# Moving the last steps of a small MLP off VectorE in a one-core decode kernel

## Chip, core and metric

The kernel runs on one core of one Trainium2 chip. The metric is the device time of one execution in microseconds (us). The kernel before takes 193.9 us, the median of three runs (193.79 to 194.43). Engines are named as in the profile: PE (TensorE matmuls), PEld (weight loads of TensorE), DVE (VectorE), ACT (ScalarE), POOL (GpSimd) and SP (SyncE, which here only issues DMAs).

## What is computed

One token with 512 features is normalised. A branch A is attention over the last 4096 positions of a cache of 32 heads with 128 features each. A branch B is a small MLP with two residual steps and a silu at its end. The result is x plus the product of both. Cut to what matters:

```python
xn = layernorm(x)                                   # 1 x 512
q  = xn @ wq                                        # 32 heads x 128
p  = softmax(q . k_cache[:, -4096:] / sqrt(128))
s  = (p . v_cache[:, -4096:]) @ wo                  # 1 x 512

x1 = xn + shift(gelu(layernorm(xn) @ w1)) @ w2      # one token: the shift leaves zeros
h2 = gelu(layernorm(x1) @ w3) @ w4
g  = silu(x1 + h2)
out = x + s * g
```

Keys, values and weights are bf16. Keys and values of the window are 32 MB each, and all bytes are read once: 78.8 MB.

## The kernel before

**Staging.** The 32 heads are worked in 8 groups of 4. A group's keys are one block of 128 partitions x 128 columns x 128 features (4 MB), as are its values. Three key blocks fit on the chip (`K_BUFS = 3`) and two value blocks (`V_BUFS = 2`). All big transfers but wq are issued by SP in program order (`load`, L75), and an issue waits until its buffer is free. The first key block comes in two halves of 64 columns, the last value block in four pieces (columns 0 to 64, 64 to 96, 96 to 112, 112 to 128, `cuts`, L570), followed by the last rows of wo (`load_rows`). The value pool is opened in the space of the pool `wts` (L580), so the first value load waits until the last reader of `wts` tiles is done; `hr` (L279) is one of those tiles.

**Scores.** The columns of a group are shared between two ways. VectorE takes the first 64 to 80 columns (`nd`) in four parts (`k_vector`): a product of keys and the spread query (L338), and a sum over features (L340). PE and ScalarE take the rest in batches: PE transposes keys (`k_turn`, L356), ScalarE copies them from PSUM (L359), and PE multiplies with the query (`k_scores`, L367). Then come own scores (L376), the maximum (`sm_max`, L381 and L383), its turning across partitions (`sm_turn`, L389, L391, L393), the exponentials (`sm_exp`, L398 to L405), the denominators (`sm_den`, `sm_rden`, L411 and L416), and the weighted values (`v_wide`, L444, with the eviction L450; turning L461 and L466). The groups overlap with a lag of two steps (`LAG`).

**Order.** From L571 on the order on PE, VectorE and ScalarE is written out by hand, step by step. In step 7 PE turns the maximum of group 6 (L389) after VectorE's L416, since both use the single buffer of the PSUM pool `ps_misc`. After the last step: the last value block is used piece by piece (`v_wide` and `v_part`, L477), the output projection of the early heads is turned and multiplied with `g_own` (`y_turn`, L556 to L561), and the last four heads follow in `y_head` (L549), sixteen small products. `g_own` is read a second time in L697, and L700 and L701 add x and store. The calls of `warm` put in matmuls of zeros whose result nobody reads.

**The MLP's end** (L269 to L296) stands ahead of that region; there a scheduler orders each engine's instructions, and it sets those of VectorE between the first products of group 0. Four row groups of PSUM collect the wide row (`hr_ps`). VectorE copies it to SBUF (`hr`, L280), PE turns it into columns with four products against `ind` (L283, f32, eight passes in the profile), VectorE adds `xn_col` (L285), ScalarE takes the silu (L287), and VectorE spreads the result over a mask, 128x16, as `g_own` (L295). `hr_ps` and `h2_ps` use the one buffer of `ps_misc`, so PE's products also wait for the copy of `hr_ps`.

Of the kernel before, what the change touches and what calls it, by code (L numbers as in the profile page):

```python
# [8 lines left out]
P = 128  # L9
BF16 = mybir.dt.bfloat16  # L10
FP32 = mybir.dt.float32
ACT = mybir.ActivationFunctionType
ALU = mybir.AluOpType
# [13 lines left out]
def kernel(  # L27
# [14 lines left out]
    nc = tc.nc  # L42
# [11 lines left out]
    KC = D // P  # L54
# [9 lines left out]
    small = ctx.enter_context(tc.tile_pool(name="small", bufs=1))  # L64
# [10 lines left out]
    def load(dst, src):  # L75
# [7 lines left out]
                        in_=A_wq.rearrange("(a b c) n -> b a (c n)", a=4, c=KC))  # L83
# [19 lines left out]
    ident_f = const.tile([P, P], FP32, name="ident_f")  # L103
# [13 lines left out]
    ind = const.tile([P, 1], FP32, name="ind")  # L117
# [28 lines left out]
    def ln_stats(src_f, tag):  # L146
# [30 lines left out]
                     start=True, stop=True)  # L177
# [23 lines left out]
    for b in range(2):  # L201
        zeros(qr[b][:])
        for c in range(KC):
            wc = wq_sb[:, c, :].rearrange("p (g a d) -> p g a d", a=G, d=Dh)
            for a in range(G):
                nc.tensor.matmul(qr[b][32 * a:32 * a + 1], lhsT=xq_bf[:, c:c + 1], rhs=wc[:, 4 * b:4 * b + 4, a, :],  # L206
                                 start=False, stop=(c == KC - 1), skip_group_check=True)
    nc.scalar.copy(out=q_row[:, 0:4, 0, :], in_=qr[0][:])  # L208
    nc.vector.tensor_copy(out=q_row[:, 4:8, 0, :], in_=qr[1][:])  # L209
    for b in range(2):  # L210
        qb_ps = ps_tr.tile([P, 4, Dh], FP32, tag="pt", name="qb_ps")
        nc.tensor.matmul(qb_ps[:], lhsT=sel[:].rearrange("k b a -> k (b a)"), rhs=q_row[:, 4 * b:4 * b + 4, 0, :],
                         start=True, stop=True)
        nc.scalar.copy(out=q_bc[:, 4 * b:4 * b + 4, :], in_=qb_ps[:])
    for b in range(2):
# [5 lines left out]
        for t in range(2):  # L221
            rows = slice(64 * t, 64 * t + 64)
            nc.scalar.copy(out=q_pair[rows, 4 * b:4 * b + 4, :, G * t:G * t + G].rearrange("p g l a -> p g a l"),
                           in_=qt_ps[rows].bitcast(BF16).rearrange("p g (a m l) -> p g a m l", a=G, l=2)[:, :, :, 0, :])
# [4 lines left out]
    for j in range(KC):  # L229
        for c in range(KC):  # L230
            nc.tensor.matmul(hs_ps[:, j:j + 1], lhsT=w2_sb[:, c, j::4],
                             rhs=shifted_bf[:, c:c + 1], start=(c == 0), stop=(c == KC - 1))
# [12 lines left out]
                            in1=r_slot[:].unsqueeze(2).to_broadcast([XR, KC, XC]), op=ALU.mult)  # L245
    xt_ps = ps_misc.tile([P, KC], FP32, tag="misc", name="xt_ps")
    nc.tensor.matmul(xt_ps[:], lhsT=r_in[:].rearrange("k a n -> k (a n)"), rhs=r_row[:], start=True, stop=True)
    xn_col = small.tile([P, KC], FP32, name="xn_col")
# [5 lines left out]
    for c in range(KC):  # L254
# [3 lines left out]
        for j, dst, w in parts:  # L258
            nc.tensor.matmul(dst, lhsT=z3_bf[:, c:c + 1], rhs=w, start=False, stop=(c == KC - 1),
                             skip_group_check=True)  # L260
# [8 lines left out]
    hr_ps = ps_misc.tile([P, KC, P], FP32, tag="misc", name="hr_ps")  # L269
    zeros(hr_ps[:])  # L270
    terms = [(shifted_bf[:, c:c + 1], w2_sb[:, c, :]) for c in range(KC)]
    for i in range(11):
        n = P if i < 10 else 96
        terms.append((a_bf[0:n, i % 3, i // 3:i // 3 + 1], w4_sb[0:n, i, :]))
    for i, (col, w) in enumerate(terms):
        r = 32 * (i % 4)
        nc.tensor.matmul(hr_ps[r:r + 1].rearrange("r j n -> r (j n)"), lhsT=col, rhs=w, start=False,
                         stop=(i >= len(terms) - 4), skip_group_check=True)
    hr = wts.tile([P, D], FP32, name="hr")  # L279
    nc.vector.tensor_copy(out=hr[:], in_=hr_ps[:].rearrange("p j n -> p (j n)"))  # L280
    h2_ps = ps_misc.tile([P, KC], FP32, tag="misc", name="h2_ps")
    for j in range(KC):
        nc.tensor.matmul(h2_ps[:, j:j + 1], lhsT=hr[:, j * P:(j + 1) * P], rhs=ind[:], start=True, stop=True)  # L283
    bv = small.tile([P, KC], FP32, name="bv")
    nc.vector.tensor_tensor(out=bv[:], in0=xn_col[:], in1=h2_ps[:], op=ALU.add)  # L285
    g_col = small.tile([P, KC], FP32, name="g_col")
    nc.scalar.activation(out=g_col[:], in_=bv[:], func=ACT.Silu)  # L287


    make_masks(16)  # L290
# [1 line left out]
    make_masks(4)  # L292
    NQ = P // XC
    g_own = small.tile([P, KC, NQ], FP32, name="g_own")
    nc.vector.tensor_tensor(out=g_own[:], in0=g_col[:].unsqueeze(2).to_broadcast([P, KC, NQ]),  # L295
                            in1=masks[4][2][:].unsqueeze(1).to_broadcast([P, KC, NQ]), op=ALU.mult)  # L296
    fold_f = const.tile([P, XC], FP32, name="fold_f")
    nc.vector.tensor_reduce(out=fold_f[:], in_=ident_f[:].rearrange("d (i t) -> d t i", t=XC), axis=AX.X, op=ALU.max)
# [7 lines left out]
                     skip_group_check=True)  # L306
# [7 lines left out]
                            op=ALU.max)  # L314
    par_t = const.tile([1 + G, PB, G], FP32, name="par_t")
    nc.vector.tensor_scalar(out=par_t[:],
                            in0=ident_f[0:1 + G, 1:1 + G].unsqueeze(1).to_broadcast([1 + G, PB, G]),
# [202 lines left out]
                                    op=ALU.add)  # L520
        ox_blk[i] = ox

    small.tile([P, 48], BF16, name="pad_rows")
    y_sum = small.tile([P, D], FP32, name="y_sum")
    small.tile([P, 32], BF16, name="pad_result")

# [205 lines left out]
```

## Time and profile before

| | |
|---|---|
| median of three runs | 193.9 us (193.79 to 194.43) |
| the profiled execution | 193.44 us |
| its span, first to last instruction | 191.6 us |
| busy: PE / DVE / ACT / POOL | 123.0 / 155.0 / 89.1 / 2.2 us |
| DMA | 79.02 MB, mean 412 GB/s |
| mean granted clock of TensorE | 0.666 |
| costliest group: L340 on DVE, 32 times | 87.6 us |
| L338 on DVE, 32 times | 46.1 us |
| L359 on ACT, 51 times | 50.0 us |
| L280 on DVE, once | 0.68 us |

The page gives the busy share of each engine in 40 equal slices of the span (4.79 us each) as digits in tenths, the chain of work that ended last, followed back from the last instruction, and groups of instructions by line. A timeline gives each instruction's start, duration, engine, line, tiles and shapes; in brackets stands how long its engine sat idle before it and what released it. For a DMA the time from issue to landing is given; landing is issue plus that time. "Room" below is the time between the landing of data and the start of the first instruction that reads it.

### The profile page before, as it was taken

To read this page: it belongs to the slowest core of one execution; us is meant where nothing else is said; L and a number is where in the kernel's file an instruction comes from. 1 tells how busy PE (TensorE), PEld (TensorE's weight loads), DVE (VectorE), ACT (ScalarE), POOL (GpSimd) and SP (SyncE) were. 2 spreads that over 40 slices of the span, in tenths; PEclk is the share of its full clock that TensorE was granted. 3 is DMA by queue.
4 is the path that set the end of the run, shared out by engine and by line. 5 is a ranking of instruction groups with operands and counts; after the bars stand their busy time and mean duration, and the time that the engine had idled before them with its cause. 6 is when DMAs were issued, how large, how long until landed. Compare 5 with 4: busy or idle time off the path is not lost.

```text
span 191.6 us, 2818 instructions
## 1 busy us (share of the span) xinstructions
PE 123.0 (64%) x1141; PEld 78.5 (41%) x1141; DVE 155.0 (81%) x187; ACT 89.1 (46%) x191; POOL 2.2 (1%) x10
## 2 busy tenths in 40 slices
PE   2545956778656069626944694566867396877983
PEld 1321316566545054414433443432653184533342
DVE  4730168999999999999999999999999999982021
ACT  2000741978587065807481737372755157653120
POOL 2110000000000000000000000000000000000000
PEclk9999695555555555855695558557655858585798
DMA  6999999999999999999999998999999999999980
GB/s 218 450 410 433 446 427 460 417 417 417 427 439 438 431 438 427 438 438 438 434 438 438 438 427 380 469 438 431 421 424 439 417 431 404 455 438 409 412 339 5
DMA packets 4621, 79.02 MB, mean 412 GB/s; under 512 B 544, under 2 KB 1152, under 8 KB 1664
## 3 DMA queue, kind: packets, MB, share of 16 engines
q1 hardware_dynamic: 4432, 74.65, 91.3%
q10 hardware_dynamic: 176, 4.20, 5.1%
q8 instruction: 9, 0.15, 0.3%
q14 instruction: 4, 0.03, 0.0%
HBM read 78.84 MB, written 0.00 MB: 411 GB/s over the span
## 4 chain that ended last, share of the span: by engine, by line
DVE 70%; PE 14%; DMA 9%; ACT 4%; issue 1%; ACTq 0%; DVEq 0%
DVE S L340 42%; DVE prod L338 21%; DMA wq_sb<-in_A_wq_dram 9%; PE ov L444 3%; PE yr_ps L543 2%; PE qr_ps L206 2%; PE pt L356 1%; DVE m L383 1%; DVE S L381 1%; PE h_ps L283 1%; PE wm L532 1%; PE ot_ps L461 1%; ACT kt L359 1%; DVE mx L391 1%; ACT L287 1%
## 5 line engine op out<-in xcount | busy, mean ns | idle before, releaser
L340 DVE TENSOR_REDUCE S<-prod 128x20 f32<-128x2560 bf16 (+2 forms) x32 | 87.6, 2736 | 1.1
L359 ACT COPY kt<-pt 128x1024 bf16<-128x1024 bf16 (+1 forms) x51 | 50.0, 1004 | 45.3 <-PE pt L356 43.6
L356 PE MATMUL pt<-ident_f,kv 128*128 128x128 f32 x202 | 47.3, 388 | 5.0 <-DMA kv<-in_A_k_cache_dram 5.0
L338 DVE TENSOR_TENSOR prod<-kv,q_bc 128x2560 bf16<-128x2560 bf16 (+2 forms) x32 | 46.1, 1442 | 2.2 <-ACT q_row L216 2.1
L356 PEld LDWEIGHTS pt<-ident_f,kv 128*128 128x128 f32 x202 | 35.0, 204 | 8.3 <-DMA kv<-in_A_k_cache_dram 6.1
L367 PE MATMUL sT<-q_pair,kt 128*128 128x8 bf16 x404 | 19.1, 171 | 15.5 <-ACT kt L359 15.3
L367 PEld LDWEIGHTS <-kt 128*128 128x128 bf16 x404 | 16.5, 106 | 26.2 <-ACT kt L359 25.1
L444 PE MATMUL ov<-kv,pT 128*16 128x512 bf16 x248 | 23.9, 551 | 0.0
L389 PE MATMUL mt_ps<-ident_f,m 128*1 128x128 f32 x8 | 3.0, 372 | 21.4 <-DVE rden L416 19.5
L405 ACT ACTIVATE pT<-S,mb 128x128 bf16<-128x128 f32 x32 | 13.9, 573 | 0.2
L450 ACT COPY ov_sb<-ov 128x512 f32<-128x512 f32 x8 | 4.7, 586 | 19.4 <-PE ov L444 19.4
L444 PEld LDWEIGHTS <-pT 128*16 128x16 bf16 x248 | 7.0, 116 | 13.9 <-issue 13.0
L389 PEld LDWEIGHTS mt_ps<-ident_f,m 128*1 128x1 f32 x8 | 0.6, 79 | 22.1 <-DVE rden L416 20.1
L376 ACT ACTIVATE own<-sT,par 128x48 f32<-128x48 f32 (+2 forms) x32 | 7.4, 352 | 3.7 <-PE sT L367 3.7
L461 PE MATMUL ot_ps<-ident_f,ov_sb 128*128 128x128 f32 x32 | 7.5, 377 | 1.8 <-ACT mb L401 1.5
L208 ACT CAST q_row<-qr_ps 128x512 bf16<-128x512 f32 x1 | 0.6, 585 | 17.0 <-PE qr_ps L206 17.0
L405 ACT ACTIVATION_READ_ACCUMULATOR pT<-S,mb 128x1 f32 x32 | 8.3, 258 | 0.0
L209 DVE CAST q_row<-qr_ps 128x512 bf16<-128x512 f32 x1 | 0.7, 691 | 9.1 <-PE qr_ps L206 9.1
L398 PE MATMUL mb_ps<-md,par_t 5*128 5x4 f32 x16 | 4.3, 334 | 5.7 <-DVE md L393 5.7
L416 DVE RECIPROCAL rden<-den_ps 128x4 f32<-128x4 f32 x8 | 1.4, 175 | 7.6 <-PE den_ps L411 7.6
L398 PEld LDWEIGHTS mb_ps<-md,par_t 5*128 5x128 f32 x16 | 3.8, 290 | 6.8 <-PE sT L367 5.4
L461 PEld LDWEIGHTS ot_ps<-ident_f,ov_sb 128*128 128x128 f32 x32 | 4.8, 188 | 2.4 <-ACT mb L401 1.9
(142 smaller groups left out, 90.7 us busy)
## 6 DMA issues: line engine op xcount, KB each, us to landing
kv<-in_A_k_cache_dram SPq DMA_DIRECT2D x7, 4096.0 KB, 30.8
kv<-in_A_v_cache_dram SPq DMA_DIRECT2D x7, 4096.0 KB, 28.6
wq_sb<-in_A_wq_dram ACTq DMA_DIRECT2D x1, 4096.0 KB, 17.4
kv<-in_A_k_cache_dram SPq DMA_DIRECT2D x2, 2048.0 KB, 25.8
wo<-in_A_wo_dram SPq DMA_DIRECT2D x1, 2048.0 KB, 28.3
kv<-in_A_v_cache_dram SPq DMA_DIRECT2D x1, 2048.0 KB, 11.3
w_sb<-in_B_w_dram SPq DMA_DIRECT2D x1, 1376.0 KB, 12.5
w_sb<-in_B_w_dram SPq DMA_DIRECT2D x1, 1280.0 KB, 18.9
```

The costliest lines, as they stand in the source:

```text
L206: nc.tensor.matmul(qr[b][32 * a:32 * a + 1], lhsT=xq_bf[:, c:c + 1], rhs=wc[:, 4 * b:4 * b + 4, a, :], start=False, stop=(c == KC - 1), sk ...
L338: nc.vector.tensor_tensor(out=prod[:, 0:m, :], in0=kn[:, rows, :], in1=q_bc[:, g:g + 1, :].to_broadcast([P, m, Dh]), op=ALU.mult)
L340: nc.vector.tensor_reduce(out=st[g]["S"][:, rows], in_=prod[:, 0:m, :], axis=AX.X, op=ALU.add)
L356: nc.tensor.transpose(pt[:, i, :], kn[:, c:c + 2, :].rearrange("p c d -> p (c d)").bitcast(FP32), ident_f[:])
L359: nc.scalar.copy(out=kts[b][:, 0:n, :], in_=pt[:, 0:n, :].bitcast(BF16))
L367: nc.tensor.matmul(st[g]["sT"][:, c:c + 2, :].rearrange("p c a -> p (c a)"), lhsT=kt[:, i, l::2], rhs=q_pair[:, g, l, :], start=(l == 0), ...
L376: nc.scalar.mul(s["own"][:, 0:m, a], s["sT"][:, 0:m, a], par[:, a:a + 1])
L398: nc.tensor.matmul(mb_ps[:], lhsT=par_t[:].rearrange("k b a -> k (b a)"), rhs=md[:], start=True, stop=True)
L405: nc.scalar.activation(out=s["pT"][:, :, a], in_=s["S"][:], func=ACT.Exp, scale=scale, bias=mb[:, a:a + 1], accum_out=s["sum"][:, a:a + 1])
L444: nc.tensor.matmul(ov[r:r + 4 * G], lhsT=s["pT"][:, c:c + 4, :].rearrange("p i a -> p (i a)"), rhs=v[:, c:c + 4, :], start=(i < 4), stop=( ...
L450: nc.scalar.copy(out=s["ov_sb"][:], in_=ov[:])
L461: nc.tensor.transpose(ot_ps[:, step * j:step * j + P], s["ov_sb"][:, j, :], ident_f[:])
```

## The change

Four steps at the end of the MLP move:

- The copy of the wide row (L280) goes from VectorE to ScalarE.
- The sum with `xn_col` (L285) is no instruction of its own any more: a product of `xn_col` with the identity opens the accumulation in `h2_ps`, and the four products against `ind` add to it.
- The silu reads `h2_ps` in PSUM instead of `bv` in SBUF; `bv` is gone.
- The spreading of g over the mask (L295) goes from VectorE to GpSimd.

A padding tile grows from 48 to 64 columns, by as many bytes as a `bv` slot of 32 bytes gave up, so that what is allocated after it keeps its place.

```diff
     hr = wts.tile([P, D], FP32, name="hr")
-    nc.vector.tensor_copy(out=hr[:], in_=hr_ps[:].rearrange("p j n -> p (j n)"))
+    nc.scalar.copy(out=hr[:], in_=hr_ps[:].rearrange("p j n -> p (j n)"))
     h2_ps = ps_misc.tile([P, KC], FP32, tag="misc", name="h2_ps")
+    nc.tensor.matmul(h2_ps[:], lhsT=ident_f[:], rhs=xn_col[:], start=True, stop=False, skip_group_check=True)
     for j in range(KC):
-        nc.tensor.matmul(h2_ps[:, j:j + 1], lhsT=hr[:, j * P:(j + 1) * P], rhs=ind[:], start=True, stop=True)
-    bv = small.tile([P, KC], FP32, name="bv")
-    nc.vector.tensor_tensor(out=bv[:], in0=xn_col[:], in1=h2_ps[:], op=ALU.add)
+        nc.tensor.matmul(h2_ps[:, j:j + 1], lhsT=hr[:, j * P:(j + 1) * P], rhs=ind[:], start=False, stop=True,
+                         skip_group_check=True)
     g_col = small.tile([P, KC], FP32, name="g_col")
-    nc.scalar.activation(out=g_col[:], in_=bv[:], func=ACT.Silu)
+    nc.scalar.activation(out=g_col[:], in_=h2_ps[:], func=ACT.Silu)
...
-    nc.vector.tensor_tensor(out=g_own[:], in0=g_col[:].unsqueeze(2).to_broadcast([P, KC, NQ]),
+    nc.gpsimd.tensor_tensor(out=g_own[:], in0=g_col[:].unsqueeze(2).to_broadcast([P, KC, NQ]),
                             in1=masks[4][2][:].unsqueeze(1).to_broadcast([P, KC, NQ]), op=ALU.mult)
...
-    small.tile([P, 48], BF16, name="pad_rows")
+    small.tile([P, 64], BF16, name="pad_rows")
```

In the order of instructions per engine nothing else moves: VectorE has three fewer, PE has the added product ahead of those of L283, ScalarE has the copy behind its last copy of the query (L223) and then the silu with its table load ahead of the first copy of keys (L359), GpSimd has one instruction more, its last.

## The prediction

> **What bounds the kernel.** I read the page first (engine shares, the 40 slices, the chain that ended last), then VectorE's timeline around the change, then the issue and landing of each transfer, and last the PE timeline of the final 30 us.
>
> ```profile
> DVE 4730168999999999999999999999999999982021
> ...
> DMA  6999999999999999999999998999999999999980
> ...
> DVE 70%; PE 14%; DMA 9%; ACT 4%; issue 1%; ACTq 0%; DVEq 0%
> ```
>
> From slice 7 to slice 34 VectorE is at nine tenths: the products L338 and sums L340 run back to back, and the chain stays on VectorE from 25.61 us (first product) to 162.75 us. So a microsecond taken off VectorE at 30 us travels to 162 us. But the DMA row is also at nine tenths up to slice 37: two resources are nearly full, and the question is which of them the end waits for. The change lies at the start of the VectorE stretch (timeline of VectorE; columns start, duration, engine, line; idle time before it in brackets):
>
> ```profile
> 27.07 2.69 DVE L340 TENSOR_REDUCE S<-prod 128x19 f32<-128x2432 bf16 x1
> 29.67 0.68 DVE L280 COPY hr<-hr_ps 128x512 f32<-128x512 f32 x1
> 30.27 1.42 DVE L338 TENSOR_TENSOR prod<-kv,q_bc 128x2432 bf16<-128x2432 bf16 x1
> 32.31 0.16 DVE L285 TENSOR_TENSOR bv<-xn_col,h_ps 128x4 f32<-128x4 f32 x1 [0.63 <-PE h_ps L283]
> 32.38 2.68 DVE L340 TENSOR_REDUCE S<-prod 128x19 f32<-128x2432 bf16 x1
> 35.40 0.18 DVE L295 TENSOR_TENSOR g_own<-g_col,mh 128x16 f32<-128x16 f32 x1 [0.33 <-ACT g_col L287]
> 35.49 1.42 DVE L338 TENSOR_TENSOR prod<-kv,q_bc 128x2432 bf16<-128x2432 bf16 x1
> ...
> 39.66 1.43 DVE L338 TENSOR_TENSOR prod<-kv,q_bc 128x2432 bf16<-128x2432 bf16 x1
> ```
>
> Three foreign instructions stand between the pairs, two of them behind waits.
>
> **Part by part: VectorE.** Undisturbed, product follows product at 39.66 - 35.49 = 4.17 us. From the first product at 25.61 the fourth would start at 25.61 + 3 x 4.17 = 38.12; it starts at 39.66. The three instructions and their two waits (0.63 and 0.33) therefore cost 1.54 us, and all of it goes: 0.49 around the copy, 1.05 around the other two. Nothing new comes onto VectorE.
>
> **ScalarE.** hr_ps is complete at 26.21 + 0.38 = 26.59 and ScalarE is free at 26.32 + 0.60 = 26.92. The copy costs what the 128x512 f32 evictions L208 and L450 cost, 0.58, and ends near 27.5 instead of 30.35. It is at no cost: ScalarE idles 6.14 us before its next copy (L359 at 33.05, waiting for PE). Behind it stand the silu (0.20; its table load of 1.28 now fits into the wait for PE, where before it stood between two kt copies) and the kt copies, which cannot start before keys are transposed.
>
> **PE.** One f32 product of 128x4 is added ahead of eight passes that take 1.86 us. Nearest row: a 128x4 f32 pair, L148 or L160, 0.43 to 0.59. With all of it PE is done by 27.5 + 0.6 + 1.9 = 30.0. Queued behind it is the first transpose L356, which needs the second half of the first key block: issued at 3.23, 28.6 to landing, so 31.83; its weights load at 31.9, 0.1 later. So the addition is at no cost, and if that cover were gone it would fall on an engine that later idles 19.5 us for VectorE's rden. SP's first value load, which waits for the last reader of the weight space (the L283 products), moves from 32.34 to about 30: worth nothing, since two whole key blocks are then still queued.
>
> **GpSimd.** No row shows a 128x16 product there. Nearest: L166, 128x1, two inputs, 0.55. Bounds: 0.3 (the 128x128 select on GpSimd, 0.29) to 16 x 0.55 = 8.8. I take 0.6; even 8.8 from 30.2 ends at 39, and g_own is first read at 186.53, so its length is free. Not free may be a clash with VectorE on memory: no row has GpSimd busy beside L338. Bounds: nothing to one L166, 0.55 (below zero is excluded: it can speed up nothing). It starts near 30.2, inside the second product (29.78 to 31.2); I take 0, since it would be GpSimd that comes second.
> The Trainium skill (SBUF — State Buffer, section "SBUF: two separate sides") says that VectorE with two SBUF inputs and a GpSimd instruction that reads SBUF exclude each other for a whole instruction, and whoever starts first holds. L338 has two such inputs; no run here shows the clash. By that rule GpSimd waits for the product if it starts second, and the sum is the same; if it starts first, that is the second rival.
>
> **How far 1.54 us travels.** Three places can eat it.
> (a) Key blocks: block 1 lands at 3.88 + 37.6 = 41.5 and is first read by VectorE at 43.84; block 6 at 113.91 + 19.8 = 133.7, read at 135.50; block 7 at 132.13 + 20.9 = 153.0, read at 155.41. With 0.1 from landing to start, the smallest room is 1.7 us: passes, just.
> (b) At 162 us the chain passes from VectorE to PE:
>
> ```profile
> 162.79 0.37 PE L389 MATMUL mt_ps<-ident_f,m 128*1 128x128 f32 x1 [1.34 <-DVE rden L416]
> ```
>
> PE waits 1.34 for VectorE, whose time before this is set by the landing of block 7; that part does not move. So 1.34 passes.
> (c) The end. The last value block comes in four pieces and then the last rows of wo. Issues (SP timeline, start first) and their landings (KB, us to landing):
>
> ```profile
> 170.49 0.59 SPq L76 DMA_DIRECT2D kv<-in_A_v_cache_dram  x1
> 171.79 0.60 SPq L76 DMA_DIRECT2D kv<-in_A_v_cache_dram  x1
> 173.07 0.48 SPq L76 DMA_DIRECT2D wo_rows<-in_A_wo_dram  x1
> ```
>
> ```profile
> kv<-in_A_v_cache_dram SPq DMA_DIRECT2D x1, 1024.0 KB, 13.2
> kv<-in_A_v_cache_dram SPq DMA_DIRECT2D x1, 512.0 KB, 14.3
> wo_rows<-in_A_wo_dram SPq DMA_DIRECT2D x1, 128.0 KB, 14.3
> ```
>
> They land at 183.7, 186.1 and 187.4, and cannot come earlier: the queue is never empty (a 4 MB block lands every 9.7 us), so an earlier issue only waits longer. Against them PE's use of them:
>
> ```profile
> 184.76 0.60 PE L444 MATMUL ov<-kv,pT 128*16 128x512 bf16 x8
> ...
> 186.12 0.54 PE L477 MATMUL oP<-pT,kv 128*128 128x4 bf16 x16
> ...
> 187.25 0.56 PE L477 MATMUL oP<-pT,kv 128*128 128x4 bf16 x16
> ...
> 188.26 0.54 PE L549 MATMUL yz_ps<-o,wo_rows 128*128 128x1 bf16 x16 [0.45 <-DVE o L492]
> ```
>
> Room, less 0.1 for the start: 184.76 - 183.7 - 0.1 = 1.0 for the second piece; 187.25 - 186.1 - 0.1 = 1.05 for the last; about 1.2 for the last four of the sixteen L549. So of 1.34 some **1.0 us** arrives; the rest turns into PE waiting for value pieces.
>
> **Sum.** The profiled execution took 193.44 (span 191.6 and 1.84 around it): 193.44 - 1.0 = 192.4. The median of the runs is 193.9, 0.46 above it. A slower execution of the same transfers has its tail later, so it has more room, not less, and the same microsecond is taken off there: **192.9**. At most the full 1.34 comes off: 192.5 to 192.6.
>
> **Rivals.**
> 1. *The clock falls in the tail (slower).* Granted clock by stretch (length, PE, PEld, DVE, ACT and POOL busy, clock, DMA share, GB/s):
>
> ```profile
> 176.40:179.80 3.40, 3.40 (x28) 0.76 (x23) 0.00 (x0) 0.00 (x0) 0.00 (x0) 0.53 0.95 400
> 179.80:183.20 3.40, 3.02 (x45) 1.47 (x41) 0.75 (x4) 0.58 (x1) 0.00 (x0) 1.00 0.99 413
> ```
>
> PE gets full clock after a stretch in which it was wholly busy, and lost it again at 152 and 163 us after stretches about half idle. The tail now runs at full clock on 3.0 of 3.4 us busy. If PE comes early and waits for value pieces, that share sinks. Price at half clock, from 183 on: the eight L444 start at landing, 183.8, and take 0.8 (32 take 3.22 at half clock); four f32 transposes 1.09 as at 157.56 instead of 0.66, twice; L477 and L549 some 0.65 each; so 183.8 + 0.8 + 1.1 + 0.65 + 1.1 + 0.25 + 0.65 + 0.4 (VectorE) + 0.65 = 189.4 for the end of L549, against 188.80 now: 0.6 slower, 0.75 if it falls one stretch earlier. Median 194.5 to 194.6. It decides once the wait brings PE's share in 180 to 183 below what holds the clock, which lies somewhere between 55% and 85%. For it: the room is used up. Against: the waits are under 1 us and lie between dense groups. Chance 0.16.
> The Trainium skill (TensorE: Matmul & The Clock Gate, section "What's actually happening") tells of a free-running activity window of 3413 ns that sets half or full clock. The trace's clock steps agree (stretches of 3.4 us); so the phase differs from run to run.
> 2. *GpSimd holds VectorE.* If silu ends before 29.78, g_own starts before the product and VectorE loses up to 0.55: 1.54 - 0.55 = 1.0 leaves (b), and a tail 0.3 later in other runs makes 193.0 to 193.5. Chance 0.10.
> 3. *Nothing arrives.* Key blocks 6 and 7 or PE's own queue at 153 to 162 hold the step, or the added products run late; 193.9. Chance 0.08. That the change does not do what it says is part of this; the instruction order shows the three gone from VectorE.
>
> **Numbers.** Forecast 0.66, at 192.9 (192.4 to 193.3). A measurement of this kernel can tell about 0.3% (0.58 us) from no change. Faster: 0.66 and half of rival 2, 0.71; same: the rest of 2, rival 3 and the edge of rival 1, 0.16; slower: 0.13. The range 192.4 to 194.1 leaves out rival 1 and a little below.
>
> **What would show it.** Right: L338 at 25.6, 29.8, 34.0 and 38.1; the copy on ScalarE at 27; mt_ps near 161.5; waits of PE for the value pieces near 183.7 and 186.1; L549 ending near 187.8. Wrong: a gap in VectorE near 30 (GpSimd); granted clock under 1.0 after 180; landings of key blocks directly ahead of L338.

## The result and the profile after

The changed kernel takes 192.40 us (median of six runs, 192.30 to 192.72) against 193.89 us (six runs, 193.67 to 194.43): ratio 0.9922, 95% interval 0.9908 to 0.9936. That is 1.5 us off, where 1.0 was forecast. Its profiled execution took 192.31 us (span 190.4), 1.1 us under the profiled execution of before.

The page of the changed kernel: the DMA row, and the chain that ended last.

```profile
DMA  6999999999999999999999999999999999999991
...
DVE 56%; DMA 32%; PE 7%; ACT 1%; issue 1%; SPq 1%; DVEq 0%; ACTq 0%
```

The DMA share of the chain went from 9% to 32%: in the last 60 us the chain runs through the landings of key block 7 and of a value piece, where before it ran through VectorE up to 162.7 us and mostly through PE after that. VectorE's timeline around the change:

```profile
25.72 1.43 DVE L338 TENSOR_TENSOR prod<-kv,q_bc 128x2432 bf16<-128x2432 bf16 x1 [2.12 <-DMA kv<-in_A_k_cache_dram]
27.18 2.69 DVE L340 TENSOR_REDUCE S<-prod 128x19 f32<-128x2432 bf16 x1
29.90 1.43 DVE L338 TENSOR_TENSOR prod<-kv,q_bc 128x2432 bf16<-128x2432 bf16 x1
...
34.08 1.43 DVE L338 TENSOR_TENSOR prod<-kv,q_bc 128x2432 bf16<-128x2432 bf16 x1
...
38.26 1.43 DVE L338 TENSOR_TENSOR prod<-kv,q_bc 128x2432 bf16<-128x2432 bf16 x1
```

Product follows product in 4.18 us; the fourth starts at 38.26 instead of 39.66, 1.40 earlier. The moved work, on ScalarE and on GpSimd (timelines of these engines):

```profile
26.64 0.59 ACT L280 COPY hr<-hr_ps 128x512 f32<-128x512 f32 x1
27.25 1.28 ACT L287 ACT_TABLE_LOAD   x1
28.59 0.17 ACT L287 ACTIVATE g_col<-h_ps 128x4 f32<-128x4 f32 x1
```

```profile
28.84 0.22 POOL L295 TENSOR_TENSOR g_own<-g_col,mh 128x16 f32<-128x16 f32 x1 [16.30 <-ACT g_col L287]
```

All of it is over before the second half of key block 0 lands at 31.8, where PE's first transpose waits. Now the end. The same three transfers as shown of before (SP timeline, start first; then KB and us to landing):

```profile
167.94 0.60 SPq L76 DMA_DIRECT2D kv<-in_A_v_cache_dram  x1
169.23 0.60 SPq L76 DMA_DIRECT2D kv<-in_A_v_cache_dram  x1
170.51 0.48 SPq L76 DMA_DIRECT2D wo_rows<-in_A_wo_dram  x1
```

```profile
kv<-in_A_v_cache_dram SPq DMA_DIRECT2D x1, 1024.0 KB, 15.5
kv<-in_A_v_cache_dram SPq DMA_DIRECT2D x1, 512.0 KB, 16.7
wo_rows<-in_A_wo_dram SPq DMA_DIRECT2D x1, 128.0 KB, 16.8
```

They are issued 2.6 us earlier and land at 183.4, 185.9 and 187.3, only 0.1 to 0.3 earlier: the time to landing grew by nearly all that the issue gained. Their use (timeline of PE and PEld):

```profile
181.10 1.04 PE L444 MATMUL ov<-kv,pT 128*16 128x512 bf16 x16 [0.27 <-DMA kv<-in_A_v_cache_dram]
...
183.53 0.61 PE L444 MATMUL ov<-kv,pT 128*16 128x512 bf16 x8 [0.40 <-DMA kv<-in_A_v_cache_dram]
...
184.76 0.47 PEld L477 LDWEIGHTS <-kv 128*128 128x128 bf16 x16 [0.28 <-DMA kv<-in_A_v_cache_dram]
...
185.99 0.56 PE L477 MATMUL oP<-pT,kv 128*128 128x4 bf16 x16
...
186.99 0.50 PEld L549 LDWEIGHTS <-wo_rows 128*128 128x128 bf16 x16 [0.54 <-DMA wo_rows<-in_A_wo_dram]
```

The first four rows each start within 0.1 us of the landing of their value piece (the first and third piece land at 167.35 + 13.7 = 181.05 and 168.59 + 16.1 = 184.69). The weight loads of L549 begin when the larger part of the last rows of wo lands (384 KB, 169.88 + 17.1 = 187.0); only the last four of the sixteen read the part that lands at 187.3. The room of about 1 us that the kernel before had is gone, and with it the part of the saving that does not show.

### The profile page after: what moved, and what is told of

Its sections match the earlier page's. It is cut to its first block, busy times and chain, and to the rows that moved or that the text cites. A ratio compares the mean times of both kernels' runs of the same rounds, so it can differ in the third digit from the quotient of the medians.

```text
span 190.4 us, 2822 instructions
## 1 busy us (share of the span) xinstructions
PE 121.9 (64%) x1143; PEld 78.4 (41%) x1143; DVE 154.3 (81%) x184; ACT 89.8 (47%) x192; POOL 2.4 (1%) x11
## 4 chain that ended last, share of the span: by engine, by line
DVE 56%; DMA 32%; PE 7%; ACT 1%; issue 1%; SPq 1%; DVEq 0%; ACTq 0%
DVE S L340 34%; DMA kv<-in_A_k_cache_dram 24%; DVE prod L338 19%; DMA kv<-in_A_v_cache_dram 8%; PE pt L356 3%; PE ov L444 1%; ACT kt L359 1%; SPq L76 1%; PE sT L367 1%; PE ot_ps L461 1%; DVE m L383 1%; DVE S L381 1%; DVE mx L391 1%; PE oP L477 1%; DVE md L393 0%
## 5 line engine op out<-in xcount | busy, mean ns | idle before, releaser
L340 DVE TENSOR_REDUCE S<-prod 128x20 f32<-128x2560 bf16 (+2 forms) x32 | 87.6, 2736 | 1.1
L359 ACT COPY kt<-pt 128x1024 bf16<-128x1024 bf16 (+1 forms) x51 | 50.0, 1004 | 43.8 <-PE pt L356 42.2
L356 PE MATMUL pt<-ident_f,kv 128*128 128x128 f32 x202 | 48.0, 392 | 11.7 <-DMA kv<-in_A_k_cache_dram 11.7
L444 PE MATMUL ov<-kv,pT 128*16 128x512 bf16 x248 | 22.7, 528 | 0.7 <-DMA kv<-in_A_v_cache_dram 0.7
L389 PE MATMUL mt_ps<-ident_f,m 128*1 128x128 f32 x8 | 3.0, 372 | 18.3 <-DVE rden L416 17.0
L450 ACT COPY ov_sb<-ov 128x512 f32<-128x512 f32 x8 | 4.7, 586 | 18.4 <-PE ov L444 18.4
L444 PEld LDWEIGHTS <-pT 128*16 128x16 bf16 x248 | 6.8, 111 | 13.3 <-issue 11.5
L461 PE MATMUL ot_ps<-ident_f,ov_sb 128*128 128x128 f32 x32 | 7.5, 377 | 1.9 <-ACT mb L401 1.6
L389 PEld LDWEIGHTS mt_ps<-ident_f,m 128*1 128x1 f32 x8 | 0.6, 80 | 18.8 <-DVE rden L416 17.4
L461 PEld LDWEIGHTS ot_ps<-ident_f,ov_sb 128*128 128x128 f32 x32 | 4.8, 188 | 2.5 <-ACT mb L401 2.0
## 6 DMA issues: line engine op xcount, KB each, us to landing
kv<-in_A_v_cache_dram SPq DMA_DIRECT2D x1, 2048.0 KB, 13.7
```

Source lines behind the costliest of these rows:

```text
L340: nc.vector.tensor_reduce(out=st[g]["S"][:, rows], in_=prod[:, 0:m, :], axis=AX.X, op=ALU.add)
L356: nc.tensor.transpose(pt[:, i, :], kn[:, c:c + 2, :].rearrange("p c d -> p (c d)").bitcast(FP32), ident_f[:])
L359: nc.scalar.copy(out=kts[b][:, 0:n, :], in_=pt[:, 0:n, :].bitcast(BF16))
L389: nc.tensor.transpose(mt_ps[:], s["m1"][:], ident_f[:])
L444: nc.tensor.matmul(ov[r:r + 4 * G], lhsT=s["pT"][:, c:c + 4, :].rearrange("p i a -> p (i a)"), rhs=v[:, c:c + 4, :], start=(i < 4), stop=( ...
L450: nc.scalar.copy(out=s["ov_sb"][:], in_=ov[:])
```

## The experiments

**Theory F** (floor): the transfers give a floor near 192.3; the kernel before ends above it by an amount that differs from run to run with the moment at which TensorE's clock becomes full; the change brings nearly all runs down to the floor. **Rival P** (passes): what VectorE saves arrives whole, and the runs differ because the transfers do. Ratios are to the kernel before, run on the same chip (medians there 194.05 for e1 to e4, 193.62 for e5, e6, e7 and e9, 193.95 for e8 and e10); a ratio is not the quotient of two medians and differs from it by up to 0.3%.

**e1, the kernel before again.**

> The kernel before, unchanged. Theory F (the changed kernel's end stands on the transfer stream, and the kernel before's on its engine chain, which scatters with the phase of TensorE's clock): median 193.9, runs spread over 0.5 us or more, last wo rows landing at 187.3 to 187.5 in this profile too whatever its span, and their first use 0.8 to 2 us after the landing. Rival P (what VectorE saves arrives whole, and the scatter is in the transfers): in a longer execution the landings are later by as much as the span is longer.

Median 194.01, runs from 192.34 to 195.19. So the spread is wider than the first runs showed, and the lowest run of the kernel before is the changed kernel's 192.3. Its profiled execution took 194.35, 0.9 longer than the first one of before. Issue and landing of its last rows, and their use (SP timeline, transfer row, PE timeline):

```profile
172.95 0.48 SPq L76 DMA_DIRECT2D wo_rows<-in_A_wo_dram  x1
```

```profile
wo_rows<-in_A_wo_dram SPq DMA_DIRECT2D x1, 128.0 KB, 14.6
```

```profile
189.16 0.54 PE L549 MATMUL yz_ps<-o,wo_rows 128*128 128x1 bf16 x16 [0.45 <-DVE o L492]
```

They land at 187.55, 0.2 later than in the first profile and just past F's 187.5; the products that read them start at 189.16, 0.9 later than there. In this execution the longer time is in the chain, not in the transfers: P's half on the scatter falls. The clock differs too (stretches of e1; after the colon stand the length and the time in which PE was busy, and the clock is the third number from the end):

```profile
174.20:177.60 3.40, 3.40 (x28) 1.44 (x28) 0.18 (x1) 1.91 (x9) 0.00 (x0) 0.50 0.95 402
177.60:181.00 3.40, 3.40 (x24) 0.82 (x23) 0.00 (x0) 0.00 (x0) 0.00 (x0) 0.50 0.99 414
181.00:184.40 3.40, 3.02 (x41) 1.52 (x37) 0.75 (x4) 0.58 (x1) 0.00 (x0) 0.99 0.99 408
```

Full clock comes at 181.0 here and at 179.6 in the first profile of before. PE was busy all through the stretch up to 177.6 as well, and full clock did not follow that one. In the changed kernel full clock comes at 176.8:

```profile
173.40:176.80 3.40, 3.40 (x25) 1.16 (x21) 0.18 (x1) 1.32 (x8) 0.00 (x0) 0.50 0.82 347
176.80:180.20 3.40, 3.02 (x40) 1.49 (x39) 0.18 (x1) 0.59 (x1) 0.00 (x0) 0.99 1.01 426
180.20:183.60 3.40, 2.48 (x31) 0.81 (x33) 0.92 (x5) 0.42 (x1) 0.00 (x0) 1.00 0.97 404
```

**e2, the copy back on VectorE.**

```diff
-    nc.scalar.copy(out=hr[:], in_=...)
+    nc.vector.tensor_copy(out=hr[:], in_=...)
```

> The change with one part undone: the wide row is copied by VectorE again, which costs VectorE about 0.5 us. Theory F: the changed kernel's PE waits 0.27, 0.40 and 0.28 us for the first three value pieces, so about 0.3 to 0.4 of the 0.5 is covered: 192.4 to 192.6. Rival P: 192.9.

192.60 (192.27 to 193.02), ratio 0.9946 (0.9926 to 0.9966). By the medians 0.2 of the 0.5 us put back on VectorE shows, as F has it; by the ratios (0.9922 and 0.9946, whose intervals overlap) all of it does, as P has it. So e2 does not decide between the two. Nor is the cover in its profile what F expected: PE waits 1.02 and 0.41 us for the first two value pieces, longer than in the changed kernel; in that profile full clock lasts to 173 us, where the changed kernel's lost it at 170, and the pieces land 0.3 later.

**e3, less VectorE time on top of the change.**

```diff
-        return 76 if g == 0 else 64 if g >= LATE else 80
+        return 76 if g == 0 else 72 if g == 1 else 64 if g >= LATE else 80
```

> The changed kernel with 8 of group 1's 80 VectorE columns given to PE and ScalarE: VectorE has 8 x (1.49 + 2.82) / 20 = 1.7 us less to do, the transfers stay. Theory F: nothing is gained, 192.2 to 192.4, and PE waits longer for the value pieces. Rival P: 190.7.

192.44 (192.23 to 192.93), ratio 0.9922 (0.9896 to 0.9947). VectorE lost another 1.7 us of work and the time is what the change alone gives. P falls. But the saving ends earlier than F has it. VectorE's work ahead of key block 6 ends 1.4 us sooner than in the changed kernel, and then it waits for that block (VectorE's timelines, the changed kernel first):

```profile
134.01 1.48 DVE L338 TENSOR_TENSOR prod<-kv,q_bc 128x2560 bf16<-128x2560 bf16 x1
```

```profile
133.99 1.49 DVE L338 TENSOR_TENSOR prod<-kv,q_bc 128x2560 bf16<-128x2560 bf16 x1 [1.29 <-DMA kv<-in_A_k_cache_dram]
```

In the changed kernel this block lands at 112.51 + 21.4 = 133.9 and VectorE reads it 0.1 later, so the change alone has used up the room there. PE waits 0.31 and 0.41 us for the first two value pieces, hardly longer than the 0.27 and 0.40 of the changed kernel: that part of F's expectation was not met. So e3 shows that the transfers hold VectorE at block 6; it does not test the value pieces.

**e4, fewer bytes on top of the change.**

```diff
-            v = load_kv(v_pool, A_v_cache, h)
+            v = load_kv(v_pool, A_v_cache, h, (0, 112) if h == 0 else (0, CP))
...
-                v_wide(h, v)
+                v_wide(h, v, 112 if h == 0 else CP)
```

> The changed kernel without the values of the last 16 of 128 columns of group 0 (they are neither loaded nor used): 0.5 MB less, so every later landing 1.2 us earlier; VectorE's work stays. Theory F: the waits for the value pieces go and the engine chain holds the end again, 191.9 to 192.1, with the runs spread wider than the changed kernel's 0.4 us. Rival P: 192.4, no gain.

192.31 (nine runs, 191.64 to 192.91), ratio 0.9939 (0.9909 to 0.9969). The median missed F's 191.9 to 192.1 and lies next to P's 192.4, and by the ratio nothing is gained; the spread came as F said, three times that of the changed kernel's six runs, with two runs at 192.0 or less, under the old floor. In the profile of its lowest run (PE timeline) the waits for value pieces are gone:

```profile
181.01 1.04 PE L444 MATMUL ov<-kv,pT 128*16 128x512 bf16 x16
...
182.86 0.60 PE L444 MATMUL ov<-kv,pT 128*16 128x512 bf16 x8
...
186.36 0.54 PE L549 MATMUL yz_ps<-o,wo_rows 128*128 128x1 bf16 x16 [0.45 <-DVE o L492]
```

A reading that fits, and is not shown by more than this: with the landings out of the way the chain scatters again, and in most runs it lies less far ahead of the landings than one profile suggested.

**e5, both of e3 and e4.**

> The changed kernel with both: 8 of group 1's VectorE columns given to PE and ScalarE (VectorE 1.7 us less), and the values of the last 16 columns of group 0 left out (0.5 MB, landings 1.2 us earlier). Theory F: the end stands on the transfers again, now 1.2 us earlier, 191.1 to 191.4, narrow spread; so of the two steps that brought 0.0 and 0.1 alone the pair brings 1.1. Rival P: 192.3, or the sum of the two alone.

191.35 (191.08 to 191.99), ratio 0.9871 (0.9838 to 0.9905): 1.0 under the changed kernel, from two steps that gave 0.0 and 0.1 alone. The spread, 0.9, is not the narrow one that F expected. VectorE reads key block 6 at 132.81, 1.2 us earlier than in the changed kernel, and the waits for value pieces are back, 1.0 us earlier (PE timeline):

```profile
180.06 1.04 PE L444 MATMUL ov<-kv,pT 128*16 128x512 bf16 x16 [0.92 <-DMA kv<-in_A_v_cache_dram]
...
182.51 0.61 PE L444 MATMUL ov<-kv,pT 128*16 128x512 bf16 x8 [0.42 <-DMA kv<-in_A_v_cache_dram]
...
185.98 0.56 PE L549 MATMUL yz_ps<-o,wo_rows 128*128 128x1 bf16 x16 [0.45 <-DVE o L492]
```

**e6, the kernel before with fewer bytes** (the edit of e4).

> The kernel before without the values of the last 16 columns of group 0 (0.5 MB less). Theory F: the engine chain, not the transfers, holds the end in most runs, so the median stays at 193.8 to 194.0; the lowest runs may fall below 192.3. Rival P (the scatter and the end are in the transfers): 192.8.

194.46 (193.35 to 194.96), ratio 1.0030 (0.9999 to 1.0062). Nothing gained: before, the transfers did not hold the end. The median lies above F's 194.0 and 0.8 above that of the kernel before on this chip, inside the spread that the kernel before shows.

**e7, the kernel before with less VectorE time** (the edit of e3).

> The kernel before with 8 of group 1's VectorE columns given to PE and ScalarE: 1.7 us off VectorE in another place, nothing of the change. Theory F: it ends where the changed kernel ends, 192.3 to 192.5, with a spread of 0.7 us or less. If the change had a gain of its own beyond VectorE's time: 193 or more.

192.61 (192.46 to 193.22), ratio 0.9938 (0.9913 to 0.9962). 1.7 us off VectorE in another place ends within 0.2 us of the change, 0.1 above F's 192.5, with a spread of 0.8. VectorE reads key block 6 at 134.09, where the changed kernel has 134.01. The change has no gain beyond VectorE's time that these runs show.

**e9, the kernel before with PE kept busy ahead of the tail.**

```diff
+            warm(2)
             ox_pick(1)
+            warm(1)
             sm_turn(NG - 1)
+            warm(1)
             sm_exp(NG - 1)
```

> The kernel before with four more matmuls of zeros in PE's waits between 171 and 174 us, so that PE is wholly busy earlier and the full clock comes earlier in the tail. If the height of the kernel before over 192.3 is in good part the moment of the full clock: 193.0 to 193.6, with fewer runs over 194.5. If it is VectorE's time alone, whatever the clock: 194.0 to 194.4, since the four add 0.3 to 0.4 us to PE.

192.52 (192.39 to 193.93; ten of twelve runs at 192.65 or less, the others at 193.76 and 193.93), ratio 0.9947 (0.9921 to 0.9972). Nothing is taken off VectorE here; four matmuls of zeros are added, and the kernel before drops to the floor in ten of twelve runs. Stretches of its profile:

```profile
172.00:174.00 2.00, 2.00 (x8) 0.63 (x7) 1.53 (x7) 0.89 (x6) 0.00 (x0) 0.50 0.95 410
174.00:176.00 2.00, 1.77 (x14) 0.67 (x13) 0.62 (x3) 0.49 (x2) 0.00 (x0) 0.69 0.96 410
176.00:178.00 2.00, 2.00 (x25) 0.77 (x29) 0.18 (x1) 1.41 (x8) 0.00 (x0) 1.00 0.96 406
```

PE is busy 3.18 of the 3.41 us up to 175.2, and there the clock becomes full, instead of at 179.6 or 181.0. The drop is larger than the 193.0 to 193.6 expected: an earlier full clock in the tail is enough to take nearly all of the height over the floor.

**e10, the change and the four matmuls.**

> The changed kernel with the same four matmuls of zeros as e9. Each alone brought the kernel before to 192.4 to 192.5. Theory F: both use up the same height over the transfers, so the two together bring nothing more: 192.3 to 192.5, the lowest run not under 192.2. Rival P (the change and the clock are separate gains, 1.5 and 1.1): 191.3 or lower.

192.46 (192.30 to 192.95), ratio 0.9929 (0.9903 to 0.9954). Two remedies of 1.5 and 1.1 us give 1.5 together: they use up the same height. No kernel here that computes the whole result went clearly below the changed one.

**e8, the spreading back on VectorE.**

```diff
-    nc.gpsimd.tensor_tensor(out=g_own[:], ...)
+    nc.vector.tensor_tensor(out=g_own[:], ...)
```

> The change with GpSimd's part undone: VectorE spreads g again. Since the silu is now done near 28.8 us, inside VectorE's sum L340, VectorE waits for nothing and pays some 0.1 us. Both theories: 192.3 to 192.5; if GpSimd's instruction had cost VectorE time by a clash, this one would be faster than the changed kernel by 0.2 or more, and its products L338 in the trace would stand closer than 4.17 us.

192.57 (192.35 to 192.70), ratio 0.9927 (0.9904 to 0.9949). VectorE's timeline:

```profile
30.25 1.42 DVE L338 TENSOR_TENSOR prod<-kv,q_bc 128x2432 bf16<-128x2432 bf16 x1
31.60 0.17 DVE L295 TENSOR_TENSOR g_own<-g_col,mh 128x16 f32<-128x16 f32 x1
31.71 2.69 DVE L340 TENSOR_REDUCE S<-prod 128x19 f32<-128x2432 bf16 x1
34.43 1.43 DVE L338 TENSOR_TENSOR prod<-kv,q_bc 128x2432 bf16<-128x2432 bf16 x1
```

It costs VectorE no time that shows in its rhythm (30.25 to 34.43 is the same 4.18), and the median lies within the spread of the changed kernel. In these runs GpSimd's part of the change is worth nothing by itself, and it costs nothing.

## Why the prediction was right or wrong, step by step

- **VectorE's 1.54: right in kind, 1.40 measured.** 0.1 of the rest is the first product, which starts at 25.72 instead of 25.61; from the first product to the fourth 1.51 us went. The row of after names key block 0 as its releaser, the row of before ScalarE.
- **ScalarE, PE, GpSimd at no cost: right.** The eight f32 passes of PE took 1.03 us at full clock instead of 1.86 at half; the copy ended 0.3 sooner and the added product was 0.2 shorter than taken, so g_own came 1.4 us earlier than worked out. g_own took 0.22, not 0.6: the row it was taken from is a power, not a product.
- **Rival 2, the clash of GpSimd and VectorE: not seen, not tried.** g_own ran from 28.84 to 29.06 beside the sum L340, which has one input, and L340 kept its 2.69. The rule of the Trainium skill (SBUF — State Buffer, "SBUF: two separate sides") speaks, among others, of VectorE instructions with two inputs in SBUF; no run here put this GpSimd product beside one.
- **(a) Key blocks: right that they let VectorE pass, and only just.** Blocks 6 and 7 were read at 135.42 and 155.33 before, not 135.50 and 155.41, so the smallest room was 1.6. After the change VectorE reads block 6 at 134.01, 0.1 after its landing, and block 7 at 153.91, 0.8 after its landing at 153.1. Block 6 had nothing left to give, as e3 shows.
- **(b) "So 1.34 passes": wrong.** L389 starts at 161.82, 0.97 earlier, since PE itself, at half clock, was late: its four transposes ahead took 1.09 where they had taken 0.64 at full clock in the profile of before. Then full clock came for the 32 products L444 of group 5 (1.90 instead of 3.22), and the eviction L450 starts 2.55 earlier, at 167.36 instead of 169.91 (PE timelines, before and after):

```profile
159.98 0.64 PE L356 MATMUL pt<-ident_f,kv 128*128 128x128 f32 x4
...
166.63 3.22 PE L444 MATMUL ov<-kv,pT 128*16 128x512 bf16 x32
```

```profile
160.48 1.09 PE L356 MATMUL pt<-ident_f,kv 128*128 128x128 f32 x4
...
161.82 0.37 PE L389 MATMUL mt_ps<-ident_f,m 128*1 128x128 f32 x1
...
165.40 1.90 PE L444 MATMUL ov<-kv,pT 128*16 128x512 bf16 x32
```

PE's part, which "does not move" in the prediction, did move: the clock first took 0.4 us of VectorE's step and then added 1.6.

- **(c) The room of 1.0 us at the value pieces: right.** 192.4 was worked out for a profiled execution; the changed kernel's took 192.31. The room decided this, and not the step that arrived: PE's L461 in the tail starts 2.15 us earlier (179.72 instead of 181.87), not 1.34, and the end moved by 1.1.
- **The sum: the step that failed.** "A slower execution of the same transfers has its tail later, so it has more room, not less, and the same microsecond is taken off there." The first half holds (e1), the second does not follow from it. Where the room is larger, more comes off: the changed kernel's runs end at the floor (e5 and e10), and what a run gains is its height over the floor. For the median that is 193.89 - 192.40 = 1.5, for the execution in e1 194.35 - 192.3 = 2.0. I set 1.34 as the most that could come off because I took one execution's wait of PE for a bound on all, and gave PE the same clock after the change as before; in the profile after, the tail's full clock came 2.8 us earlier. The forecast should have been the floor, 192.4, with its bound above, not the median less one microsecond.
- **Rival 1, the clock falls in the tail: did not happen.** In the stretch 180.2 to 183.6 PE was busy 2.48 of 3.40 us (73%) with waits for value pieces, and the clock stayed full to the end. The profile's busy share gives no clean limit: full clock was kept after 61% (after, 112.0 to 115.4) and lost after 66% (before, 114.7 to 118.1). The loss at 152 came after a stretch only 28% busy, not half. The same clock mattered on the other side: e9 shows that an earlier full clock is enough to take the kernel before to the floor in most runs, and e7 that less VectorE time is enough too. The Trainium skill (TensorE: Matmul & The Clock Gate, "What's actually happening") has full clock follow a window of 3.4 us in which PE is busy, with windows that run on whatever the kernel does. The traces agree on the windows: in the profile of before the clock steps from 77 us on lie on one grid of 3.41 us to within 0.02 us. On what is busy enough they agree only in part. Full clock came at 176.8, 179.6 and 181.0 in three profiles, each time after a stretch with PE busy all the time; but it did not follow e1's stretch of 174.2 to 177.6, just as busy, and in the profile of before it followed one of 89%:

```profile
165.94:169.35 3.41, 3.03 (x36) 1.27 (x40) 3.34 (x3) 1.32 (x5) 0.00 (x0) 0.50 0.96 413
169.35:172.76 3.41, 1.89 (x20) 0.88 (x8) 2.70 (x7) 2.38 (x10) 0.00 (x0) 1.00 0.96 413
```

What stays open: which part of the changed kernel's gain in a given run is VectorE's 1.4 and which the earlier clock that follows from it. The two are not separate, since an earlier tail meets the windows at another place; e7 and e9 show only that either suffices. Nor was it tried whether the phase of the windows alone explains every run of before. The runs fit it: many that show the same mean granted clock took nearly the same time (0.670: four runs, 195.08 to 195.22; 0.687: seven, 194.27 to 194.55; 0.655: nine, 193.58 to 193.93), though at 0.679 two took 192.4 to 192.5 and five 194.8 to 195.0. A higher mean does not go with a shorter time. What makes a stretch busy enough for full clock is open. So is which landing holds the floor in a given run, that of key block 6 for VectorE or those of the value pieces for PE: no run moved one without the other.

## What to carry to other kernels

Where one stream of transfers runs without a gap, work out first the end that its last landings allow, and set each run's height over it: a gain is that height, and no more, whichever engine it comes from. Do this for every landing that an engine waits for: here key block 6 had become as tight as the end. A spread of runs whose lowest meets that floor says that the chain above it varies; forecast the floor for the median, not the median less a fixed saving. A profile is one phase of TensorE's clock: before a tail that PE sets, ask what would bring the full clock earlier, since four matmuls of zeros in PE's waits did here, in ten of twelve runs, nearly what the whole change did.

## What was not expected of the hardware

The kernel before ran between 192.3 and 195.2 us, a spread of 1.5%, while the last rows landed within 0.2 us of each other in its two profiles; e9 took ten of twelve runs to 192.4 to 192.65 with four matmuls of zeros. A GpSimd product of 128x16 f32 took 0.22 us, less than its power of 128x1 (0.55). Full clock held through a stretch with PE busy 73%, while PE busy 2.72 of 3.40 us (before, 172.8 to 176.2) did not bring it, and neither did 3.40 of 3.40 (e1, 174.2 to 177.6).
